# A third wide product in seven products of quarters, a weight loaded in halves, and a new instruction order

## The chip, the cores and the metric

The kernel runs on one core of a Trainium2 chip. The metric is the device time of one execution in microseconds. The core's engines are PE (matmul), DVE (vector), ACT (scalar), POOL (GpSimd, which here issues most loads) and SP (which issues stores and turning transfers).

## The reference

A recurrent retention layer is followed by a mixer over tokens and channels. B = 4 batches, H = 8 heads, S = 768 tokens, D = 64; the model width is 512, and the token and channel layers are 256 and 1536 wide. All inputs and the output are float32.

```python
gamma = 1.0 - 2.0 ** (-5.0 - np.arange(H))
for t in range(S):
    state = gamma * state + np.einsum('bhd,bhe->bhde', k[:, :, t], v[:, :, t])
    y[:, :, t] = (1 / np.sqrt(D)) * np.einsum('bhd,bhde->bhe', q[:, :, t], state)
x = y.transpose(0, 2, 1, 3).reshape(B, S, H * D)
h = np.maximum(x.transpose(0, 2, 1) @ w_tok1, 0.0) @ w_tok2
u = x + h.transpose(0, 2, 1)
out = u + np.maximum(u @ w_ch1, 0.0) @ w_ch2
```

## The kernel before, in words

Everything is held on the chip in 16-bit floats where matmuls read it. The work has two parts.

The **front** goes over 16 units, a batch b and a pair of heads p. The recurrence is cut into six chunks of 128 tokens. k and q are scaled by powers of the decay (L528 on ACT, L530 on DVE), turned by PE (L552, L554; the turned q of batch 0 and a few others is scaled at L562 with a table made at L433) or by a transfer on SP (L542). PE multiplies k and v into chunk states (L584), DVE runs the recurrence over the chunks (L594, L596), and the states go to the `cross` tiles (L614 on ACT, L616 on DVE). Scores (L635) are masked by DVE (L646, 128 x 384 at a time), and y is the masked scores times v (L666) plus the cross part (L692). Banks are evicted to 16 bits at L708 on ACT or DVE. The two token products are L723 and L743, with a rectification between them on ACT (L732) or DVE (L734). The result u is turned (L788 or a transfer at L778) into `uT`.

The **back** goes over batches. The wide product, u times w_ch1 with rectification, has two forms. `widen` makes 12 x 2 blocks of four matmuls over 384 tokens (L822), each rectified by ACT (L838). `widen7` splits both operands into quarters and makes seven products in place of eight: four differences of uT on DVE (L861), four sums of the weights made once, and then for each of six blocks seven products of two matmuls (L891), three copies of partial banks (L902, ACT or DVE), three additions on DVE (L911) that are rectified in place (L915, DVE), and one last rectification straight from the bank (L942 on ACT or L944 on DVE). The set `WIDE7` says which batches take this form; before, they are 2 and 3. The narrow product, with w_ch2, takes seven products for all batches (L1005 sums on DVE, L1041 and L1051 products, L1031 copies, L1058 additions), except the last half of batch 3, which is plain (L967, L976). Stores are issued at L982 and L1084.

The order is not found at run time. A planner (`arrange`) reads two strings: `ORDERED` names every operation once, in the sequence in which it is put on its engine, and `WAYS` says for operations that two engines can do which of them takes it (0 the first named, mostly ACT, 1 DVE). The class `Rings` models transfers with a time per descriptor, a first delay and a delay until landing; its numbers settle the order in which the emitted instructions of different engines and the banks are arranged. Each engine then runs its own instructions strictly in that order. Loads are all on POOL's queue except the first k, in the sequence that the string gives; from the seventh load on, a load waits for the one six places ahead of it. While the plan shows PE waiting in the first 21 us, filler matmuls on zeros are emitted (L1164).

The second token weight (256 x 768) is one load of two row tiles and is waited for by both halves j of the product at L743:

```python
t2 = op(one("PE", (335, 500), emit), [hr, wops["t2"], x_ops[j]], [], [H1, Y[j]])
```

Of the kernel before, what the change touches and what calls it, by code (L numbers as in the profile page):

```python
# [38 lines left out]
class Rings:  # L39
# [28 lines left out]
    def step(self, landed):  # L68
        dt, t = self.DT, self.t
        on = [(q, l[0]) for q, l in self.line.items() if l and l[0][2] <= t]  # L70
        if on:
            round_ = sum(x[0].dma[1] for _, x in on)
            for q, x in on:
                n = dt / round_
                if x[3] > t:
                    n = min(n, dt / self.GEN[q])
                x[1] -= n
                if x[1] <= 0:
                    self.line[q].pop(0)
                    landed.append((x[0], t + dt + self.land(q, x[0], t)))  # L80
        self.t = t + dt
# [9 lines left out]
def arrange(ops, BUFS, BANKS, seq, ways):  # L91
# [162 lines left out]

ORDERED = (
    "0b0d000a08050e0107020c2423040j060f292a030i2b250927260h282h2i2k0g332c2m342j0l352l37362d0k2e47382f2o2g0m43482q"
    "2n443h3i3k0n493l454a4b463m0q392p4c3a4h0o3j534d2r3b4k544e2s4i3c4f3d0p2t4j4g3e4l3f0s572u4m553g4n583n564o4p3p3o"
    "3q3r5i3s0u5l2v2y5m2w3t4r2x0v2z593u4q5a305h5b3v0t4s5c3y5d3w4t5e5j5f0w6763644u315k5g5o4v0r3z3x5n5p325q4w855r40"  # L260
    "0x4y4x86415s654z5t420z6650515u6894520y5v955y5w69115z6h5x76606j61hm1362hj6lij6ahn6k12hkim7372hp6b6ihlik106chq"
    "hsil6d77hrht74hois6e75786fithu79in7a147g7bioi4iu7jj16g7c6n7ihvhw7h6mj27ki5177d6oi77ei6iy6q1zhyhx6pi86rja21j3"
    "jgjh7f18206si9jijb6ti11c8182iv6ujciz6v6xig226yidi26w15hzi3iwi0jdihix83ia84ibj41aj01viej5iiip6z1w70j616j7icje"
    "if1yjn711987jj7m7o88iqjljo7lj81gjkir7nkb89j91xjfjp9z1b8ajukc7pjqaxjs8b1e7q8cjv8fk5jt8djy8i908gjw91k77r8hjxa0"
    "kgjm7s8ja18ek1khb0b18k7tjz8mk28l7u8njr7w1fb2k0a57x96kr8okk1d7v97ksk98pkl7y1h9892a6kaa28q93k61ukv99a78ra87z9a"
    "kwa9kea3809ba4aa8sk89cl0ay8tkt9eazkf9d8v9gkil19f8wkx9i8x9h8u9jl4kjctku9l9kky9m9n1ib3kdkn9ob4abb58ycu1sb69p8z"
    "b7kol21jb89qbvl5byadackz1ml39rag9u9sl9ae1t9vafl69wah9t9xl7bb9yaiajbfakal1nldbcamlelaanmdbdljbzmempc0mfaolfb9"
    "maapcvlkban4mqbeaqmrn5arcwbhm1bwbjasatbxllbgbiaumy1kmbn6kqavczc1mc1om2bkc2m7c3mzd0bldrmjepn0m8c4d1m3mkl8bmm9"
    "mlcxd2lyeq1lcybnmvkmlzlg1rd3bolbc5d4mwawbpbrmxlhbqm4k4dsm5k3bsc6mglibtlvm0lsd5m6c9eslmcdlwfnmhcblxlnlpcalolq"
    "ccltlrc7d7lummc8d8msd6mtcfdbmnn1etmod9njeumuminankn7ndcedtn2da1pn8nbnen9cgo5duncnfn3ddcidfcholevcjdxo6ordydv"  # L270
    "dzckdwe0glosnhewfoexe1noerclningdcnmey1qnpe2decmomnncpdgnlopcnezdhf0nqgmcqoonscrcsconrondie3ntoqfpnvf1djf2e5"
    "nwbuoufqe4e6dke8ovdnlce9dloynye7dmkpf3donzozowotdqdpf7eaebo1edeco3oxeef6p0eff4frf5ftegnuf9fup3o0nxeho4fso2f8"
    "faeip4o8p7ejp6p1fcfbgro7ekoafvo9fwfdgsocp9gtelfxodobfegup2ohffp8gooegvemoifgfyeneoofpbfhgwfjogpcpsfzfig1ptpg"
    "g4fkpdg5pxphpipepypjg2pzpkq0papufmplq1pqg0qqq2pngxpvgnq7q4flpoq9q8q5qgqrqxg3qaqvgyprqsqwqeqbqtqfqygpr7qcqzqh"
    "gqg6r0g8qir5gag7r2qjokr6g9ror3gbqlr9r8qmrercr1rppfqorardrqqdojrtpmr4rfqururrgcrgq3rwrhrvrxrmripwgdrjryqps3rn"
    "rbgerss4rzghqks0rkgfthtdgitjgjtfgktis1gggztesvh1tmh2srtoh0sws9tntph3h4tqqnssh6h5rlh7h8stt0q6h9tkt2t1tltrtss2"
    "tghattpptvtuhbt4s5hcs6t5hfhdt3sxs7hgt6s8sahihhsehet7sysbp5susgsfszsiscsht9t8sjsksdtbtzsnslsmu3uku0u4u5ulsoum"
    "u1u8upunu9uau6uqurubu2ustaucviutv8uduiuoufuuuzuguwv1vjuxvktwvnv2uvv3tyuevovlv6spvpv4v7vqtxv0vzvrv9wnvsvavxuj"
    "v5w1vbvuvywgvvvdvgvmw0vew6vhytw4w2whylwiu7w5w3wlvcuhymwjw7wmy5uyw8vwwowky6w9wpwevtwbwqwfwvvfsqwswrwcxnwwwtx1"
    "wdwuwaynxpxjxkyoxox3wxypxsxlx2wyyqxuxtxqxmxwx4x6wzxxxvx8x7xyx9yrydx0xaxzxcy0xby7x5y3y8xdysxfxetcy1xgxhy9xiy2"  # L280
    "yaxryey4yfybygyhyiycyuyvywyjyxyyykyzz0"
)
WAYS = (
    "000000000000000000000000000000000000000000000000000000000000000000000000000100000000000010000000000000100001"
    "001000000000000000000000000000000001101000000000000000000000000100100000100000000000000000000000000000000100"
    "001100000000000100000000000000011000001000000000001000000000000000000000010000000000000000000000000000000000"
    "000000000000000000000000000000000010001100000000000000000000010100000010010000000010000000000001001001011011"
    "000000010000000000100100100001100100000001100000000000000000000110110000000000000000000000000000010011000000"
    "010000000000000000100001001000000000000000000000000000000010010000000010000000000000000000000000000000000000"
    "000000000000000000000000000000000000000000000000000000000000000000000000000100000000000000000000011000000000"  # L290
    "000000000001100000000000000000000000000000000000000000000000000000000000000000000000000000000000000000000110"
    "000000000000000000001000000000000000000001100000000000000000000000000000000000000000000000000000000000001000"
    "000000000000000000000000000000000000000000000000000100000000010000000000000000000000100000000000000000000110"
    "000000000000000000000000000000000000000000000000000000000000000100000000000000000000000000000000000000000000"
    "0000000100000000011000000000000000000001000000001000000010000000100000001"
)


# [1 line left out]
def kernel(  # L300
# [74 lines left out]
    def one(eng, cost, emit):  # L375
        return [(eng, cost[0], cost[1], emit)]
# [122 lines left out]
    def front(b, p):  # L499
# [238 lines left out]
        for j in range(2):  # L738
            def emit(j=j):
# [62 lines left out]
    def back(b):  # L802
# [150 lines left out]
        def narrow(sh, blocks=range(HC)):  # L953
            H2, rel = H2s[sh], rels[sh]
            for i in blocks:
# [3 lines left out]
                for cols in cuts:  # L959
# [20 lines left out]
                    def emit(e, sh=sh, i=i, cols=cols):  # L980
                        t0 = (sh * HC + i) * P
                        (nc.sync if e == "SP" else nc.scalar).dma_start(out=out[b, t0:t0 + P, cols], in_=X.tile[:, sh * HC + i, cols])  # L982
                    op(either(emit, ACT=(380, 101), SP=(450, 100)), [ad], [], [X], dma=(8, 90 * w_ // C))


        def narrow7(i0, i1):
# [95 lines left out]
            for i, d in ((i1, [o21, o22]), (i0, [o11, o12])):  # L1082
                def emit(e, i=i):
                    (nc.sync if e == "SP" else nc.scalar).dma_start(out=out[b, i * P:(i + 1) * P, :], in_=X.tile[:, i])  # L1084
                op(either(emit, ACT=(380, 101), SP=(450, 100)), d, [], [X], dma=(8, 90))
# [8 lines left out]
        for f in steps:  # L1094
# [1 line left out]
            part[0] += 2  # L1096


    ORDER = ("q00 k00 q01 v00 k01 k02 k03 v01 v02 q02 q03 t1 t2 v03 k10 q12 q10 k11 q13 q11 a0 v10 a1 v11 "
             "a3 a2 b1 b2 b0 k12 v12 k13 v20 v13 k20 q20 q21 v21 k21 k22 k23 v22 q22 q23 v23 k30 v30 q30 "  # L1100
             "k31 v31 q31 v33 v32 k33 q32 k32 q33").split()
    for what in ORDER:
        n = int(what[1])
        if what[0] in "kqv":
            load(n, int(what[2]), what[0])
        elif what == "t1":
            weight("t1", 48, 40, wt1, moe_w_tok1)
# [36 lines left out]
    for b in range(B):  # L1144
        back(b)

    seq = [int(ORDERED[2 * i:2 * i + 2], 36) for i in range(len(ORDERED) // 2)]
# [49 lines left out]
```

## Time and profile before

| | |
|---|---|
| median of 3 runs | 189.81 us (189.17 to 190.44) |
| profiled execution | 190.01 us |
| its span, first to last instruction | 188.2 us |
| busy PE / DVE / ACT / POOL | 181.2 / 166.5 / 124.2 / 52.8 us |
| mean granted clock of PE | 0.999 |

Busy time counts an instruction from start to end, and the next one on the engine can start before that end; so the sum of single durations is larger than the busy time, and a matmul row that is busy all the time does not say that the matmuls run at their peak. The rows are read by line number of the kernel, as in the description above; `L822 PE MATMUL ... x192 | 36.0, 326` means 192 matmuls of line 822, 36.0 us busy together, 326 ns from start to end of one.

### The profile page before, as it was taken

The numbers are of one execution on the slowest core, as the hardware profiler recorded it, in microseconds if no ns is written. First come the engines' busy times: TensorE is split into PE (matmuls) and PEld (weight loads), VectorE is DVE, ScalarE is ACT, GpSimd is POOL, SyncE is SP. The second block draws the span as 40 slices with busy tenths as digits, with TensorE's granted clock in tenths as the row PEclk, the third lists the DMA queues.
The fourth block names the chain that finished last, engine by engine and source line by source line (L and its number), as shares of the span: only waits on it lengthen the run. The fifth ranks groups of instructions, "written<-read, shape, count | busy, mean of one in ns | idle before, by whom it ended". The sixth has DMA issues, their size and how long they took to land.

```text
span 188.2 us, 5284 instructions
## 1 busy us (share of the span) xinstructions
PE 181.2 (96%) x2109; PEld 136.7 (73%) x2109; DVE 166.5 (88%) x448; ACT 124.2 (66%) x282; POOL 52.8 (28%) x62
## 2 busy tenths in 40 slices
PE   7989999999999999999999899999999999999993
PEld 3455888667688988776668788965678986567872
DVE  3789999997889999958799989999999999999982
ACT  3965989569889898478663686598883444575100
POOL 7995686536440708405202200000000000000000
PEclk9999999999999999999999999999999999999999
DMA  9999999999999999999999979724312031121045
GB/s 122 155 157 196 179 188 177 208 191 201 159 155 144 125 155 122 147 136 163 195 163 127 115 99 251 158 43 86 98 56 45 0 101 56 72 98 59 0 177 215
DMA packets 91977, 24.92 MB, mean 132 GB/s; under 512 B 81968, under 2 KB 89008, under 8 KB 91952
## 3 DMA queue, kind: packets, MB, share of 16 engines
q0 software_dynamic: 67456, 13.18, 85.3%
q1 hardware_dynamic: 23776, 10.10, 24.5%
q10 hardware_dynamic: 720, 1.31, 1.9%
q8 instruction: 16, 0.26, 0.6%
q14 instruction: 9, 0.07, 0.1%
HBM read 26.74 MB, written 6.29 MB: 175 GB/s over the span
## 4 chain that ended last, share of the span: by engine, by line
PE 78%; DVE 12%; DMA 3%; ACT 2%; issue 2%; POOL 1%; SPq 0%; POOLq 0%; ACTq 0%; DVEq 0%
PE bank L822 16%; PE bank L891 15%; PE bank L1041 14%; PE bank L1051 10%; PE bank L743 5%; DVE am L646 4%; PE bank L723 4%; PE bank L635 3%; PE bank L967 3%; DMA kT<-k 3%; DVE U L596 2%; PE bank L666 2%; PE bank L692 2%; DVE qT L562 2%; PE bank L584 1%
## 5 line engine op out<-in xcount | busy, mean ns | idle before, releaser
L822 PE MATMUL bank<-uT,wc 128*128 128x384 f16 x192 | 36.0, 326 | 0.0
L646 DVE TENSOR_TENSOR am<-bank,mask 128x384 f16<-128x384 f32 x64 | 33.2, 549 | 1.7 <-PE bank L635 1.5
L838 ACT ACTIVATE h<-bank 128x384 f16<-128x384 f32 x48 | 21.5, 500 | 10.3 <-PE bank L822 10.3
L490 POOL DMA_DIRECT2D v<-in_v_dram x16 | 16.4, 1031 | 40.0 <-PE bank L692 17.9
L822 PEld LDWEIGHTS <-wc 128*128 128x128 f16 x192 | 17.2, 98 | 9.1 <-DVE X L708 0.2
L902 ACT COPY us<-bank 128x384 f32<-128x384 f32 x34 | 15.5, 481 | 8.9 <-PE bank L891 6.4
L1041 PEld LDWEIGHTS <-hs 128*128 128x128 f16 x198 | 18.5, 98 | 3.0 <-issue 0.7
L1031 ACT COPY us<-bank 128x256 f32<-128x256 f32 x31 | 11.8, 384 | 13.3 <-PE bank L1041 13.0
L911 DVE TENSOR_TENSOR h<-bank,us 128x384 f16<-128x384 f32 x36 | 19.3, 553 | 1.1 <-PE bank L891 0.4
L1058 DVE TENSOR_TENSOR X<-X,bank 128x256 f32<-128x256 f32 x44 | 17.9, 414 | 2.2 <-PE bank L1051 1.4
L1041 PE MATMUL bank<-wsum,hs 128*128 128x256 f16 x132 | 17.9, 273 | 0.6 <-ACT us L1031 0.6
L596 DVE SCALAR_TENSOR_TENSOR U<-U,gp,bank 128x64 f32<-128x64 f32 x64 | 17.1, 281 | 0.7
L708 ACT CAST x<-bank 128x384 f16<-128x384 f32 x30 | 14.1, 492 | 5.0 <-PE bank L692 5.0
L490 POOL DMA_DIRECT2D k<-in_k_dram x15 | 15.4, 1035 | 5.3 <-DVE U L596 1.7
L708 ACT CAST u<-bank 128x384 f16<-128x384 f32 x28 | 13.2, 489 | 3.4 <-PE bank L743 3.2
L891 PE MATMUL bank<-hs,late 128*128 128x384 f16 x72 | 14.9, 326 | 0.0
L743 PE MATMUL bank<-h,wt 128*128 128x128 f16 x192 | 14.7, 219 | 0.0
L891 PEld LDWEIGHTS <-late 128*128 128x128 f16 x96 | 9.0, 98 | 6.4 <-issue 0.4
L1051 PEld LDWEIGHTS <-h 128*128 128x128 f16 x132 | 12.5, 98 | 1.6
L614 ACT ACTIVATE cross<-U,gp 64x320 f16<-64x320 f32 x23 | 12.8, 560 | 1.2 <-DVE U L596 0.7
L723 PE MATMUL bank<-x,wt 128*128 128x128 f16 x192 | 13.3, 219 | 0.0
L743 PEld LDWEIGHTS <-wt 128*128 128x128 f16 x192 | 11.9, 98 | 1.6
(89 smaller groups left out, 374.2 us busy)
## 6 DMA issues: line engine op xcount, KB each, us to landing
out_dram<-X SPq DMA_DIRECT2D x18, 256.0 KB, 2.4
v<-in_v_dram POOLq DMA_DIRECT2D x16, 192.0 KB, 6.7
q<-in_q_dram POOLq DMA_DIRECT2D x16, 192.0 KB, 7.3
k<-in_k_dram POOLq DMA_DIRECT2D x15, 192.0 KB, 7.2
wc<-in_moe_w_ch_dram POOLq DMA_DIRECT2D x5, 512.0 KB, 13.4
out_dram<-X ACTq DMA_DIRECT2D x5, 256.0 KB, 2.1
wt<-in_moe_w_tok_dram POOLq DMA_DIRECT2D x2, 384.0 KB, 9.1
wc<-in_moe_w_ch_dram POOLq DMA_DIRECT2D x2, 256.0 KB, 9.0
```

Of the source, the lines that this page charges most:

```text
L490: (nc.sync if hard else nc.gpsimd).dma_start(out=tile_of(s, [P, 2, NC, D], FP if hard else F16), in_=src.rearrange("h (c p) d -> p (h c) d ...
L596: nc.vector.scalar_tensor_tensor(out=u[:, c], in0=u[:, c - 1], scalar=gp[:, p:p + 1], in1=st, op0=ALU.mult, op1=ALU.add)
L646: nc.vector.tensor_tensor(am, SC[g].tile[:, :m * P].rearrange("p (i t) -> p i t", t=P), mask.to_broadcast([P, m, P]), ALU.mult)
L708: (nc.scalar.copy if e == "ACT" else nc.vector.tensor_copy)(tile(), t)
L723: nc.tensor.matmul(acc[:, jt * P:(jt + 1) * P], wt1[:, i, jt * P:(jt + 1) * P], X16.tile[:, i].rearrange("p h d -> p (h d)"), start=(i == ...
L743: nc.tensor.matmul(Y[j].tile[:, 2 * i * D:2 * (i + 1) * D], wt2[:, jt, t], H1.tile[:, jt], start=False, stop=(jt == NJ - 1), skip_group_ch ...
L822: nc.tensor.matmul(acc[:, :SH], wc1[:, ct, ft * P:(ft + 1) * P], UT.tile[:, ct, sh * SH:(sh + 1) * SH], start=(ct == 0), stop=(ct == NP - 1))
L838: nc.scalar.activation(H2.tile[:, ft], A.tile[:, :SH], AF.Relu)
L891: nc.tensor.matmul(acc[:, :SH], left(ct), r[:, ct], start=first and ct == 0, stop=ct == C2 - 1, skip_group_check=True)
L911: nc.vector.tensor_tensor(h(m, sh), R.tile[:, :SH], KS.tile[:, j], ALU.add)
L1041: nc.tensor.matmul(acc_[:, lo], l[:, j], r[:, j], start=first and j == 0, stop=j == K2 - 1, skip_group_check=True)
L1051: nc.tensor.matmul(acc_[:, lo], l[:, j], r[:, j], start=first and j == 0, stop=j == K2 - 1, skip_group_check=True)
```

## The change

`WIDE7` becomes (1, 2, 3), so batch 1's wide product is made by `widen7`. The second token weight is loaded by two transfers of 384 columns each (`t2a`, `t2b`), and half j of the product waits for its own. The transfer model gets other numbers: a landing delay for ACT's queue, 700 instead of 1000 ns more for turning transfers, other landing delays for POOL's loads, POOL's share of the transfer engines fixed at 0.6 while a hardware queue is active, and 130 instead of 90 ns per descriptor of a store. `ORDERED` and `WAYS` are replaced as a whole (1296 operations in place of 1261; the two characters of an operation now count to base 62).

```diff
-    LAND = dict(SP=900, ACT=2000)
+    LAND = dict(SP=900, ACT=900)
-    LATER = 1000
+    SOFT = 0.6
+    LATER = 700
...
-            return 1470 if t < 6000 else 2900 if t < 13500 else 2300
+            return 1470 if t < 4500 else 2100 if t < 17000 else 1700 if t < 30000 else 2000
...
-            round_ = sum(x[0].dma[1] for _, x in on)
+            hard = len(on) - ("POOL" in dict(on))
             for q, x in on:
-                n = dt / round_
+                share = (self.SOFT if hard else 1.0) if q == "POOL" else (1.0 - self.SOFT if hard < len(on) else 1.0) / hard
+                n = share * dt / x[0].dma[1]
...
-    WIDE7 = (2, 3,)
+    WIDE7 = (1, 2, 3,)
...
-            t2 = op(one("PE", (335, 500), emit), [hr, wops["t2"], x_ops[j]], [], [H1, Y[j]])
+            t2 = op(one("PE", (335, 500), emit), [hr, wops["t2" + "ab"[j]], x_ops[j]], [], [H1, Y[j]])
...
-                    op(either(emit, ACT=(380, 101), SP=(450, 100)), [ad], [], [X], dma=(8, 90 * w_ // C))
+                    op(either(emit, ACT=(380, 101), SP=(450, 100)), [ad], [], [X], dma=(8, 130 * w_ // C))
...
-        elif what == "t2":
-            weight("t2", 16, 150, wt2, moe_w_tok2)
+        elif what[:2] == "t2":
+            half = slice(0, SH) if what == "t2a" else slice(SH, S)
+            weight(what, 16, 64, wt2[:, :, half], moe_w_tok2[:, half])
```

Read by number, the two orders differ in these places that the prediction speaks of. POOL's queue begins with v, q of the first unit, then k, q of the second, the iota of the decay table, q of the third; afterwards it begins with q, v of the first unit, that iota, then q, k, v of the second. DVE makes all constants before the first scaling of k. The first weights of the wide product stand behind two more loads of batch 1 (its first v and second k). Choices between engines: of 48 scalings of k and q, 26 were on DVE and 13 are; of 96 evictions at L708, 14 and 8; of 16 rectifications between the token products, 5 and 1; the last rectifications of `widen7`, 0 of 12 and 4 of 18; two copies of partial banks leave DVE. The last operations of the old order are plain narrow products in slices, the last of 128 columns, each with its store; in the new order these slices come earlier, and the last are a chain of seven-product matmuls, its addition and the store of a whole block of 128 x 512.

More of the change, by code (lines that the diff above doesn't have):

```diff
@@ L262 @@
[L262 to L266, printed above, removed]
@@ new lines @@
+    "1Y1z1q250n2o1r2s2p261B0k242q2t1A2u1C2r2v1D0p1Z2C2w201E2E2F0q2Y2x2D271F210r2y292G282Z2b2z2a2H0w2c342A1G2d3035"
+    "2B360t2I1H1J2e311I0s371K32382f392J1L332K2g2M0v2L1M3a2h2j2N1N3c0u2k2O3e2i3y2l3d3f0A4K2P3b3h3C3g3i3z3k2m3D0x3m"
+    "3j3l2Q3n2T4L0y2R3E3o2U3F3G2n5j0z3p47483q2V3t3H3r2W2S0D493u3I3A2X3v3w3J3saf0B3x3Bac5kadaMaeaN4aagaO3M4b3K3Q0C"
+    "ax3Naoap3Oay3Paq0EarazaV4caWahasaX0F3S4l3Lal4nat4d4o3R3T4eb74m3Vai4f0G3U4gaj4pamb84haG4ib9aD1aakauaE3WaA1c0L"
+    "avaHaw1b3XaFaJ3Y1daKaBaL3Z4j0JaIba4042bj4143bgaCaY4kanbk44bhbmb4bl0K1645bd46aZ18bb0Ibibeb54G4H4qbnaPbc174s0O"
@@ new lines @@
+    "bfb1b0aQaS19aR4M0Hb6b24I4Nb34OaTbo4ubO0Nbp4J4r4Pbq5f4QbPbsaU0M4Rbr4SbI4U5O4t4Wbv0R4v4Ybxbw4V5g4w0S4X4T6pbzbJ"
+    "5Pby500P4x5h6UbAbBbL5ibt4ZbK4y6q0Q5152bu4zbE534A5lc45U54bMbC6m5m5n4B6V5VbFbT5R5W5o555XbN5p4C5YbUbR5q6n5rbXbD"
+    "4Dc85Z56bYbS5S5tc5c95T5s575ucd585w4E5Qc7cebV595v4F5abQ6rchc6bW5x5y5Aci60c06o5C615b5z5BbZ0T6s5Dcm7sc16t5E0W5c"
+    "6u7tc36vcf7ucn5F0U6w626xcg6y5G636W155J5H645dcj655Kc25I66675L5Mck695e6A5N686bcl6aca6c6B6Xcqcu7v6dcb6EcvcLcc6e"
+    "cw6zcrcNcs6fcMcz6C6gcQ7wcA6i6DcBcRcOcC6Y70cxcDcT0Z6Zct6jcScU6GcEcJ6h0X6IcVcGcKcPd26k71cHcX0V80dR72cYd4d3dT73"
@@ new lines @@
+    "12dScyd7d57yd8dUdWd97zdVdXda7AcF6F746HdbdZ7B11756Jd07CdcdYe0dh6K7D13cIde76e1e6df6L14e7did1dj6Me3dkcW78e48y6Q"
+    "7983dA7adodBdl8zdpdC7b8AdF77dmdrdG7cdHdsdqbGdD7d7EdI7xdtdydJdE7edn7ge5dz6N0YdubHdK81dPdvdd6Oe2dM82dLdQd67fdw"
+    "867Feyeu6RdNeU6Pew7heWev7i6SeF87cZez88eQ847jeG85eDdxdg7kdO96eSeJ99896leReAeEeX9a7leK7oeB9b7meH8a8b7nex7G8ceT"
+    "f1eI8d7KeM7J7pf2eVee7r7qeN97e8eZef8B7Mco7If58C98eCf07H8e7O8gf3cp8i8D7L7NeLf4ec107Pf6f87Q6Te9ed8f8E7R8hf98j8l"
+    "7Seaeh9E8Feg8k8n8mf77Tei7WeY7Uej8G8oeb7X9cekel7V7Z9d7Y8H9een9fem8I9F9g8peo9G8Jeq9h8qep8K8Meres8L8r8Q8u8s8P8N"
@@ new lines @@
+    "8t9k8vfcfg8wfx8O8xfhfdfzfy8R9o8T9Hfl9mfC8V8SfAfm8UfifefD9K8W9lfofF9nfp8Xfj9ifn9Lff8YfEfGfqfv9Ig5fHfsfw9JfMft"
+    "fJfNfQ9MfKg6fOg79NfPfBga9O9pfRfTgb8Z9PfU9jgdeOgcg89Q9qfWfu90ge9r92fXfVgf9t9sgkfY93gh9uglg39591g0gi949vg1g4gm"
+    "9R9wgDfkgnfI9SgEgr9TgIgs9U9xgKfZ9y9WgugJgFfSg9gtgv9VgL9zgwgBgM9XfrgogggCgN9ZgSa1gpgygT9YgOa0gx9Agza2gPhChGhE"
+    "a3hHhDhNgQa49BhLgRgGhIhOhMgqgHa5fLhghPhFhkhihQa6a8g2hJhrgAa9hhhlhUabhKgjhRhsaahp9DhVhSgYgUhqhmhTgVh0gZa7gWh3"
+    "9Ch1hjhvh4hnh5hwhohth2h6h7gXh9huh8hxhyhahchAhYhbi2ijhZi3i4hdikj8i0i7iohzi8ili5hBipiqimiahfi9i1etibirePiAicis"
@@ L1084, in emit @@
                     (nc.sync if e == "SP" else nc.scalar).dma_start(out=out[b, i * P:(i + 1) * P, :], in_=X.tile[:, i])
-                op(either(emit, ACT=(380, 101), SP=(450, 100)), d, [], [X], dma=(8, 90))
+                op(either(emit, ACT=(380, 101), SP=(450, 100)), d, [], [X], dma=(8, 130))
         if b in SEVEN:
@@ L1102 @@
     for what in ORDER:
-        n = int(what[1])
+        n = int(what[1:2])
         if what[0] in "kqv":
@@ L1145 @@
         back(b)
-    seq = [int(ORDERED[2 * i:2 * i + 2], 36) for i in range(len(ORDERED) // 2)]
+    digit = {c: i for i, c in enumerate(DIGITS)}
+    seq = [digit[a] * 62 + digit[c] for a, c in zip(ORDERED[::2], ORDERED[1::2])]
     asked = set(o.n for o in queue)
```

50 lines of the change are left out of this document (18 added, 32 removed).

## The prediction

> **What bounds the kernel now.** I read the page's span and chain, then the busy time in five stretches that I cut at the first useful matmuls of a stage, then groups and timelines for the price of one instruction.
>
> ```profile
> span 188.2 us, 5284 instructions
> PE 78%; DVE 12%; DMA 3%; ACT 2%; issue 2%; POOL 1%; SPq 0%; POOLq 0%; ACTq 0%; DVEq 0%
> ...
> 0.00:10.00 10.00, 8.54 (x63) 4.35 (x64) 5.30 (x37) 6.50 (x11) 8.86 (x15) 1.00 1.27 140
> 10.00:33.40 23.40, 21.87 (x402) 17.48 (x401) 22.36 (x53) 18.68 (x38) 16.72 (x21) 1.00 1.86 180
> 33.40:78.40 45.00, 44.88 (x557) 34.94 (x555) 41.03 (x102) 35.84 (x82) 20.19 (x20) 1.00 1.92 161
> 78.40:156.50 78.10, 77.42 (x877) 60.01 (x875) 71.07 (x189) 51.32 (x125) 7.06 (x7) 1.00 0.78 115
> 156.50:188.20 31.70, 28.44 (x218) 19.94 (x215) 26.70 (x69) 11.92 (x28) 0.00 (x0) 1.00 0.26 96
> ```
>
> The columns are the stretch and its length, then PE, weight loads, DVE, ACT, POOL, clock, DMA share and GB/s. The profiled execution took 190.01 us, 1.8 above its span, and lies 0.2 above the median 189.81. Three regimes are to be seen. Until 33.4 us DVE is the full engine (22.36 of 23.40) and PE is kept busy by filler (39 matmuls, 10.1 us, row below). From 33.4 to the end PE is full (44.88 of 45.00, then 77.42 of 78.10). The granted clock is 1.00 throughout. So matmul time removed after 33.4 us counts in full as long as DVE and ACT keep up. DVE is close behind: from 78.4 to 156.5 us it is idle for 7.0 us only, ACT for 26.8.
>
> ```profile
> L822 PE MATMUL bank<-uT,wc 128*128 128x384 f16 x192 | 36.0, 326 | 0.0
> L1164 PE MATMUL bank<-zero 128*128 128x384 f16 x39 | 10.1, 411 | 1.1 <-DVE zero L1155 1.1
> L911 DVE TENSOR_TENSOR h<-bank,us 128x384 f16<-128x384 f32 x36 | 19.3, 553 | 1.1 <-PE bank L891 0.4 <-ACT us L902 0.2
> L915 DVE TENSOR_SCALAR h<-h 128x384 f16<-128x384 f16 x36 | 7.6, 251 | 0.0
> L838 ACT ACTIVATE h<-bank 128x384 f16<-128x384 f32 x48 | 21.5, 500 | 10.3 <-PE bank L822 10.3
> L646 DVE TENSOR_TENSOR am<-bank,mask 128x384 f16<-128x384 f32 x64 | 33.2, 549 | 1.7 <-PE bank L635 1.5
> L528 ACT ACTIVATE k<-k,gk 128x384 f16<-128x384 f16 x17 | 10.0, 613 | 2.5 <-DMA kT<-k 2.2
> L902 ACT COPY us<-bank 128x384 f32<-128x384 f32 x34 | 15.5, 481 | 8.9 <-PE bank L891 6.4 <-DVE h L911 2.5
> ...
> 33.41 3.58 PE bank L822 x22
> 94.92 0.87 ACT L838 ACTIVATE h<-bank 128x384 f16<-128x384 f32 x2 [0.16 <-PE bank L822]
> 8.85 1.12 ACT L528 ACTIVATE k<-k,gk 128x384 f16<-128x384 f16 x2
> 142.10 1.01 DVE L646 TENSOR_TENSOR am<-bank,mask 128x384 f16<-128x384 f32 x2
> 139.09 0.76 DVE L915 TENSOR_SCALAR h<-h 128x384 f16<-128x384 f16 x4
> 67.80 0.32 DVE L530 TENSOR_SCALAR k<-k,gk 128x384 f16<-128x384 f16 x1
> 68.03 0.55 DVE L1005 TENSOR_TENSOR hs<-h 128x768 f16<-128x768 f16 x1
> ```
>
> **Steps, not durations.** An engine starts its next instruction before the last has drained, so I price by the step from start to start. A 384-column matmul: 3.58 us for 22 in the chain, 0.163. A DVE instruction over 128x384 from a bank: two take 1.01 and one 0.55, 0.46 to 0.47; the in-place rectification L915: (0.76 - 0.25) / 3 = 0.17; a decay L530: 68.03 - 67.80 = 0.23. On ACT an eviction: 0.87 - 0.50 = 0.37; a decay: 1.12 - 0.61 = 0.51.
>
> **The change, part by part.**
>
> *The wide product of batch 1.* It goes from 12 x 2 blocks of 4 matmuls (96) to 6 blocks of 7 products of 2 (84). All have 384 columns, so PE loses 12 x 0.163 = 1.96 us. DVE gains 4 sums and 18 additions at 0.47 and 18 rectifications at 0.17: 10.3 + 3.1 = 13.4 us. ACT loses 24 evictions (8.9) and gains 18 copies (6.7).
>
> *The engine choices.* Read number by number, the second string takes 13 decays, 6 evictions, 4 small rectifications and 2 copies from DVE to ACT, and puts 4 rectifications and a few turned tiles on DVE. Over the kernel DVE gains about 8.4 us of steps and ACT about 7.5.
>
> *The stretch in which it falls.* From the first wide product of batch 1 to that of batch 3 both orders hold the same work but for the exchange, so they can be set side by side. PE: 77.6 us of steps before and 75.7 after (the trace's stretch is 78.1). DVE: 67.1 before; +8.4 additions, +3.0 rectifications, +1.4 sums, +0.9 last rectifications, -2.7 for 12 decays, -1.9 for 4 evictions, -1.9 for 4 of the cross tiles and -1.1 for small ones give 73.3. ACT: 45.8 to 53.8. With PE's saving the stretch would be 76.1 us, of which DVE must step 96.3%. Has it done that? In the two rows below DVE was busy for 9.53 and 9.94 of 10 us while PE was full, 97.4%.
>
> ```profile
> 110.00:120.00 10.00, 10.00 (x158) 8.51 (x156) 9.53 (x24) 6.96 (x19) 0.00 (x0) 1.00 0.86 188
> 120.00:130.00 10.00, 10.00 (x99) 7.26 (x98) 9.94 (x27) 8.28 (x21) 0.00 (x0) 1.00 0.42 94
> ```
>
> The loss to a late DVE is therefore 0 at best. By busy time, where drains count, it is 7.0 idle - 6.2 added - 1.96 shorter = 1.2 us too little. I take +0.5, with 0 and +1.2 as its ordinary ends; beyond them lies the first rival. What waits on a late DVE: in a block the fourth product waits for an addition to free its bank, and later blocks take banks that the additions and ACT's copies release, so PE stops with a few blocks' lag.
>
> *The front.* Here DVE decides. The new order loads q of the first head pair first on POOL's queue, moves the second iota ahead of the next loads, makes the constants first and turns k and q before the first state product.
>
> ```profile
> 5.28 0.53 DVE L530 TENSOR_SCALAR k<-us,gk 128x384 f16<-128x384 f32 x1
> 5.62 2.50 ACT L433 ACTIVATE late<-us,lnsc,lnh 128x384 f32<-128x384 f32 x4
> 6.51 0.80 DVE L416 TENSOR_SCALAR ident<-away 128x128 f16<-128x128 f32 x1
> 8.43 0.96 DVE L562 TENSOR_TENSOR qT<-bank,late 128x768 f16<-128x768 f16 x1 [0.49 <-PE bank L552]
> 9.82 0.56 DVE L646 TENSOR_TENSOR am<-bank,mask 128x384 f16<-128x384 f32 x1 [0.43 <-PE bank L635]
> ```
>
> The decay table L433 starts at 5.62 because its iota stands behind four loads; in the new order it stands behind two, and the scaling L562 at 8.43 could start about 0.9 earlier. Against that the second pair's k is issued one load later (three take POOL 3.05 us in a row shown with the last rival, so about 1 us each), and a decay of it waiting on ACT holds the next copies: up to 1.5 us the other way. DVE's steps before the first wide product are nearly equal (27.2 and 27.5). I take -0.7, ends -0.9 and +1.5.
>
> *The second token weight in halves.* One more issue on POOL (L470, some 0.8 us, its rows below) delays the loads behind it by that. Its cover is the lead of those loads: the first wide product starts at 33.41 and its first weights were issued at 18.71, with 9.0 us to landing. They land by 27.7, a lead of 5.7 us. In the new order they stand behind two further loads of 192 KB, at the stretch's 180 GB/s 2.2 us. That is inside the lead: cost 0, and if the cover goes +0.8.
>
> ```profile
> 18.71 0.77 POOL L470 DMA_DIRECT2D wc<-in_moe_w_ch_dram  x1 [1.35 <-DMA wt<-in_moe_w_tok_dram]
> wc<-in_moe_w_ch_dram POOLq DMA_DIRECT2D x2, 256.0 KB, 9.0
> ...
> 182.26 2.68 PE L967 MATMUL bank<-wc,h 128*128 128x512 f16 x24
> out_dram<-X SPq DMA_DIRECT2D x18, 256.0 KB, 2.4
> out_dram<-X SPq DMA_DIRECT2D x2, 64.0 KB, 1.8
> ```
>
> *The end.* Before, PE ends on narrow slices (L967) and the last store is one of 64 KB, 1.8 us to landing. The new order ends on a seven-product chain, a 256-column addition and a whole 256 KB block, 2.4 us. That is +0.6 for the store and +0.1 for the addition: +0.7, ends 0 and +1.0. The new costs in the transfer model (stores, landing) act only through the order.
>
> **Sum**, on the profiled span: 188.2 - 1.96 - 0.7 + 0.5 + 0.7 = 186.7; with 1.8 around it 188.5, and 0.2 less against the median: **188.3 us**, 0.8% below 189.81. About 1% is what a measurement of this kernel tells from no change, so that forecast lies just inside it.
>
> **Rivals.**
>
> *DVE becomes the bound (slower).* Place: 78 to 156 us. In the old stretch DVE was busy for 91% (71.07 of 78.10). If its chains (addition, rectification, the next sum) allow no more than that, 73.3 us of steps need 80.5, 4.4 more than PE's 76.1. It decides from a share below 96.3%. Sum: 188.2 - 1.96 - 0.7 + 0.7 + 4.4 + 1.6 = 192.2. For it: all spare DVE time of the stage is spent. Against: the two rows above.
>
> *Nothing comes of it.* DVE loses the 1.2 and the front gains nothing: 188.2 - 1.96 + 1.2 + 0.7 + 1.6 = 189.7. For it: in 10 to 33.4 us DVE had one idle microsecond, so an earlier start may only meet later loads.
>
> *Stalls go as well (faster).* The old trace has one costly order: ACT stands 2.25 us for a turned k, and a copy queued behind it holds PE.
>
> ```profile
> 98.80 5.15 DMA kT<-k
> 104.05 1.12 ACT L528 ACTIVATE k<-k,gk 128x384 f16<-128x384 f16 x2 [2.25 <-DMA kT<-k]
> 105.47 0.82 PE L1041 MATMUL bank<-wsum,hs 128*128 128x256 f16 x6 [0.60 <-ACT us L1031]
> ```
>
> If the new transfer costs place it better and DVE keeps up: 188.3 - 0.6 - 0.5 = 187.2, with the front at its end and a free tail 186.3. Against it: 13 more decays now stand on ACT, each such a place.
>
> *Decay and rectification against POOL.* A decay usually takes 0.31 us on DVE, but up to 0.81.
>
> ```profile
> 73.44 3.05 POOL L490 DMA_DIRECT2D k<-in_k_dram  x3
> 73.76 0.81 DVE L530 TENSOR_SCALAR k<-k,gk 128x384 f16<-128x384 f16 x1
> 78.40:100.00 21.60, 21.60 (x227) 14.55 (x225) 17.11 (x47) 14.82 (x35) 5.53 (x6) 1.00 1.42 164
> ```
>
> The slow one ran while POOL issued three loads. The 18 new rectifications are of the same form and now fall where POOL still issues, as none did before. At 0.5 us each and POOL busy for 5.53 of 21.60 us, about a quarter, that is 18 x 0.25 x 0.5 = 2.3 us on DVE, 190.6 in all; the 13 decays that leave DVE give part back. The Trainium skill (SBUF — State Buffer, Who interferes with whom) says that such one-input DVE instructions in a two-port mode and GpSimd's descriptor writing take a shared port from each other for a whole instruction; this row agrees, while other decays beside POOL's issues took 0.3.
>
> **Chances.** The forecast with its own range 187.4 to 189.2: 0.47, of which 0.15 is below the 1% mark. Stalls go as well: 0.22, all below it. Nothing: 0.12. The DVE bound: 0.14, of which 0.11 beyond 1%. POOL's port: 0.05, of which 0.01 beyond. Faster by over 1%: 0.37; within: 0.51; slower: 0.12. The range, 186.2 to 191.6, leaves out the worst of the DVE bound and the best of the stalls.
>
> **What would show it.** Right: 96 matmuls left of L822's form and 252 of L891's; the stretch from the first wide product of batch 1 to that of batch 3 near 76.5 us with DVE busy above 95% and PE waiting under 1.5 us for DVE; the first mask multiplication at or before 9.3 us, the first wide product by 33; a last store of 256 KB. Wrong: PE waiting for additions or copies by several us in that stretch (DVE bound), the first wide product after 34 us (late loads), L915 above 0.4 us in the mean (port), or ACT waits on turned tiles longer than 2 us.

## The result and the profile after

The changed kernel takes **190.74 us** (median of 20 runs, 188.91 to 194.09) and the kernel before 189.22 (20 runs, 188.84 to 190.44). The ratio is 1.0045 with a 95% interval of [1.0024, 1.0066]: 0.45% slower, within the 1% called no change, where the forecast 188.3 was a gain. Four executions of the changed kernel, each over 1.5% above its fastest, are left out of the ratio; without them its median is **190.07 us**, and later medians are set beside that. The profiled execution took 191.62 us, 1.55 above 190.07; its span is 189.8, its mean granted clock 0.994. So the profile is one of the longer executions. Seven of the twenty took 188.91 to 189.53, and no profile is of one of those. Every line number of the front and of `widen7` is now three higher (L822 is L825).

The page of the changed kernel, span and chain by engine; then its busy time in stretches cut as before (stretch, length, PE, weight loads, DVE, ACT, POOL, clock, DMA share, GB/s):

```profile
span 189.8 us, 5308 instructions
PE 75%; DMA 8%; ACT 5%; POOL 5%; DVE 3%; issue 1%; SPq 0%; POOLq 0%; ACTq 0%
```

```profile
0.00:32.95 32.95, 30.12 (x449) 21.26 (x450) 27.94 (x94) 23.23 (x48) 25.89 (x36) 1.00 1.64 169
32.95:80.50 47.55, 45.26 (x574) 35.18 (x573) 42.81 (x101) 37.00 (x85) 18.68 (x19) 1.00 1.92 151
80.50:156.60 76.10, 75.92 (x859) 58.18 (x857) 74.61 (x205) 60.30 (x144) 9.10 (x9) 1.00 0.95 104
156.60:189.80 33.20, 28.97 (x224) 20.60 (x222) 27.20 (x71) 11.81 (x27) 0.00 (x0) 0.97 0.34 128
```

The third row is the one that the forecast was about: 76.10 us long where the old was 78.10, DVE busy for 98% of it, PE full. The second is the surprise: it was 45.00 us long with PE busy for all but 0.12; now it is 47.55 with PE idle for 2.29. In the chain DMA has gone from 3% to 8%.

The costly groups of the changed kernel (busy us, mean ns of one, idle before):

```profile
L825 PE MATMUL bank<-uT,wc 128*128 128x384 f16 x96 | 17.7, 326 | 0.0
L894 PE MATMUL bank<-hs,late 128*128 128x384 f16 x108 | 22.5, 326 | 0.1
L894 PE MATMUL bank<-uT,wc 128*128 128x384 f16 x72 | 15.6, 326 | 0.0
L894 PE MATMUL bank<-uT,late 128*128 128x384 f16 x36 | 8.8, 326 | 0.0
L894 PE MATMUL bank<-hs,wc 128*128 128x384 f16 x36 | 8.6, 325 | 0.0
L914 DVE TENSOR_TENSOR h<-bank,us 128x384 f16<-128x384 f32 x54 | 28.9, 550 | 1.2 <-ACT us L905 0.4 <-PE bank L894 0.2
L918 DVE TENSOR_SCALAR h<-h 128x384 f16<-128x384 f16 x54 | 12.2, 264 | 0.0
```

The change does what it says: 96 wide matmuls are left and 252 (108 + 72 + 36 + 36) stand in seven-product chains, 12 fewer in all. The rectification takes 264 ns against 251.

**Where the 2.3 us of this execution went.** The timeline of the changed kernel around 72 us, SP's and POOL's queues and PE's row after the stop:

```profile
66.95 2.46 SPq L545 DMA_TRANSPOSE qT<-q  x1
69.46 1.27 SPq L545 DMA_TRANSPOSE kT<-k  x1
70.78 1.28 SPq L545 DMA_TRANSPOSE qT<-q  x1
72.11 5.97 SPq L545 DMA_TRANSPOSE kT<-k  x3
...
71.74 1.01 POOL L493 DMA_DIRECT2D v<-in_v_dram  x1 [9.80 <-PE bank L695]
72.74 1.08 POOL L493 DMA_DIRECT2D q<-in_q_dram  x1
73.81 1.01 POOL L493 DMA_DIRECT2D k<-in_k_dram  x1
74.81 1.03 POOL L493 DMA_DIRECT2D q<-in_q_dram  x1
...
79.04 0.51 PE L638 MATMUL bank<-qT,kT 64*128 64x128 f16 x12 [2.24 <-DMA kT<-k]
```

Its chain of waits and its list of waits at this place:

```profile
72.11 6.89 DMA kT<-k
```

```profile
PE bank L638 <- DMA kT<-k: 2.2, 1, 2.2
```

SP's own longest wait is the other half of it, with the DVE instruction that it waited for:

```profile
SPq L545 <- DVE q L533: 65.7, 1, 65.7
```

```profile
66.53 0.32 DVE L533 TENSOR_SCALAR q<-q,gy 128x384 f16<-128x384 f16 x1
```

SP's queue stands until 66.95 before a q whose scaling DVE makes at 66.53. The 65.7 us of the row run from SP's first load on, for that q is next on its queue. With that q six turning transfers of batch 2 go out one behind the other, 1.3 to 2.5 us apart. The k of the second head pair is the fourth, issued at 72.11; it takes 6.89 us to land, beside a store of ACT and four loads that POOL issues between 71.74 and 75.8 after its own queue has stood for 9.80 us. PE's scores of that pair wait 2.24 us for it, and everything behind them on PE with them. Before, the same stage turned fewer tiles at a time and from 60 us on (DVE scaled that q at 60.82); SP's queue there, and the time to landing of the four k turned from 55 to 84 us:

```profile
60.01 2.09 SPq L542 DMA_TRANSPOSE kT<-k  x1
62.21 6.10 SPq L542 DMA_TRANSPOSE qT<-q  x2
68.37 1.28 SPq L542 DMA_TRANSPOSE kT<-k  x1
```

```profile
kT<-k SPq DMA_TRANSPOSE x4, 3.1
```

The same row of the changed kernel:

```profile
kT<-k SPq DMA_TRANSPOSE x4, 8.3
```

The Trainium skill (DMA: Bandwidth & Descriptors, Queues, rings and completion order) says that each transfer engine takes turns between the queues it has work for. The rows fit this but do not show the turns themselves: the k issued at 69.46 landed after 2.84 us, the one issued at 72.11, beside the loads and the store, after 6.89.

### The profile page after: what moved, and what is told of

It is laid out like the page before. It is cut to its first block, busy times and chain, and to the rows that moved or that the text cites. A ratio compares the mean times of both kernels' runs of the same rounds, so it can differ in the third digit from the quotient of the medians.

```text
span 189.8 us, 5308 instructions
## 1 busy us (share of the span) xinstructions
PE 180.3 (95%) x2099; PEld 135.2 (71%) x2099; DVE 172.5 (91%) x470; ACT 132.3 (70%) x300; POOL 53.7 (28%) x63
## 3 DMA queue, kind: packets, MB, share of 16 engines
q10 hardware_dynamic: 1152, 1.77, 2.5%
## 4 chain that ended last, share of the span: by engine, by line
PE 75%; DMA 8%; ACT 5%; POOL 5%; DVE 3%; issue 1%; SPq 0%; POOLq 0%; ACTq 0%
PE bank L894 17%; PE bank L1044 14%; PE bank L1054 10%; PE bank L825 8%; PE bank L746 5%; PE bank L726 5%; DMA k<-in_k_dram 5%; DMA kT<-k 4%; PE bank L638 3%; PE bank L970 3%; ACT us L905 2%; PE bank L669 2%; PE bank L695 2%; DVE h L914 2%; POOL v L493 2%; PE bank L587 2%
## 5 line engine op out<-in xcount | busy, mean ns | idle before, releaser
L905 ACT COPY us<-bank 128x384 f32<-128x384 f32 x54 | 24.8, 482 | 8.0 <-PE bank L894 5.1
L914 DVE TENSOR_TENSOR h<-bank,us 128x384 f16<-128x384 f32 x54 | 28.9, 550 | 1.2 <-ACT us L905 0.4
L1034 ACT COPY us<-bank 128x256 f32<-128x256 f32 x30 | 11.2, 375 | 16.7 <-PE bank L1044 15.2
L894 PE MATMUL bank<-hs,late 128*128 128x384 f16 x108 | 22.5, 326 | 0.1
L894 PEld LDWEIGHTS <-late 128*128 128x128 f16 x144 | 12.7, 98 | 7.6 <-issue 0.5
L825 PE MATMUL bank<-uT,wc 128*128 128x384 f16 x96 | 17.7, 326 | 0.0
L599 DVE SCALAR_TENSOR_TENSOR U<-U,gp,bank 128x64 f32<-128x64 f32 x64 | 16.3, 273 | 0.6
L894 PE MATMUL bank<-uT,wc 128*128 128x384 f16 x72 | 15.6, 326 | 0.0
L531 ACT ACTIVATE k<-k,gk 128x384 f16<-128x384 f16 x22 | 13.3, 619 | 2.5 <-DMA k<-in_k_dram 2.2
L894 PEld LDWEIGHTS <-wc 128*128 128x128 f16 x108 | 10.1, 98 | 5.9 <-issue 0.3
L711 ACT COPY X<-bank 128x384 f32<-128x384 f32 x29 | 13.7, 500 | 0.2 <-DVE u L711 0.2
```

The lines of the kernel that those rows point to most:

```text
L599: nc.vector.scalar_tensor_tensor(out=u[:, c], in0=u[:, c - 1], scalar=gp[:, p:p + 1], in1=st, op0=ALU.mult, op1=ALU.add)
L711: (nc.scalar.copy if e == "ACT" else nc.vector.tensor_copy)(tile(), t)
L825: nc.tensor.matmul(acc[:, :SH], wc1[:, ct, ft * P:(ft + 1) * P], UT.tile[:, ct, sh * SH:(sh + 1) * SH], start=(ct == 0), stop=(ct == NP - 1))
L894: nc.tensor.matmul(acc[:, :SH], left(ct), r[:, ct], start=first and ct == 0, stop=ct == C2 - 1, skip_group_check=True)
L905: (nc.scalar.copy if e == "ACT" else nc.vector.tensor_copy)(ks[:, j], R1.tile[:, :SH])
L914: nc.vector.tensor_tensor(h(m, sh), R.tile[:, :SH], KS.tile[:, j], ALU.add)
```

## The experiments

Each edit is against the changed kernel if nothing else is said. The characters of the order string stand for operations, two for each.

**The two kernels again, unchanged.**

> The kernel before, unchanged, looked at once more. Its first profile took 190.01 us where the median of 20 executions is 189.22, and held a stop of 0.8 to 1.0 us on PE at 104.2 to 105.5 us behind a turning transfer of 5.15 us. Theory 'transfers decide the odd microsecond': an execution near 189.2 us has that transfer at about 3 us and PE stops under 0.3 us at that place. Rival 'the stop is part of the order': the stop is there again at 0.8 us or more in an execution of 189.2 us.

> The changed kernel, unchanged, looked at once more. The profiled execution (191.62 us) stopped PE for 2.4 us at 76.6 us, for a turned k that took 6.9 us. Theory 'collision': the time of an execution follows that stop, so one of 189.0 to 189.5 us has a stop of under 0.5 us there and one above 191 us of 2 us or more; the stretches after it are the same within 0.3 us. Rival 'DVE is the bound': the stop is the same size whatever the time, and the difference lies between 80 and 157 us, where DVE is full.

Measured: 190.54 us (span 188.8) and 191.82 us (span 190.0). The starts of the first matmuls of each stage cut the profiled executions into these parts (us; W is the first wide product of batch 0, at L822 or L825, w1 and w3 those of batches 1 and 3):

| kernel | start to W | W to w1 | w1 to w3 | w3 to last matmul | to the end |
|---|---|---|---|---|---|
| before, first profile | 33.25 | 45.01 | 78.21 | 28.25 | 3.49 |
| before, second | 34.58 | 45.01 | 77.45 | 28.25 | 3.49 |
| after, first | 32.78 | 47.71 | 76.81 | 27.99 | 4.55 |
| after, second | 33.51 | 47.11 | 76.82 | 28.00 | 4.58 |

PE's stop of about 2 us ahead of L638 is in both profiles of after (2.24 and 1.6 us in the waits) and in none of before. What the old trace had of its own, the stop of 0.6 us behind ACT's turned k at 104 us (0.76 by the stretch), is not in its second profile. Yet that second execution is the longer one: PE waits 1.2 us for the first token weight (L723), and the front takes 34.58 us. Neither of the two executions lies near its kernel's median, so what was expected of one that does is not decided by them. An old execution put together from the parts without these two stops is 33.25 + 45.01 + 77.45 + 28.25 + 3.49 = 187.45 us and 1.8 around it, 189.25: that is the median of 189.22. The forecast's base, 189.81 from three runs, was 0.6 too high, and its profile held a stop that the second profile lacks.

**loads_early**: three POOL loads ahead of the one that waits.

```diff
-    "...5BbZ0T6s5Dcm7sc16t5E0W5c"
-    "6u7tc36vcf7ucn5F0U6w626xcg6y5G636W155J...
+    "...5BbZ0U0W150T6s5Dcm7sc16t"
+    "5E5c6u7tc36vcf7ucn5F6w626xcg6y5G636W5J...
```

> Three loads of batch 3 (k and q of the first pair, q of the last) are taken ahead of the load of v that stood on POOL's queue for 9.8 us, so that they run while the transfer engines are nearly idle (66 to 71 us) and not in the burst from 71.7 us on beside the turned k. Theory 'collision with the loads': the turned k takes about 3 us, PE's stop at 76.6 us goes from 2.4 to under 0.5 us, and the median falls from about 190.5 to 188.7 to 189.2 with a spread of under 1 us. Rival 'the turns hold each other': the k still takes above 5 us and the median stays above 190. Rival 'DVE is the bound': the stop goes, and what it gave comes back as waits after 80 us, median above 190.

Measured: 190.37 us (189.54 to 191.77), ratio to before 1.0039 [1.001, 1.0067]. In its profile the k of the second pair takes 5.2 us instead of 6.9, and no PE wait on it is listed; but that execution took 189.72, and the median is no lower than 190.07. Taking the burst away shortens the transfer, it does not bring the time back.

**turns_late**: two of the six turns (k of the fourth and third pair, `7u`, `6W`) behind a store on SP.

```diff
-    "6u7tc36vcf7ucn5F0U6w626xcg6y5G636W155J5H645dcj655Kc25I6...
+    "6u7tc36vcfcn5F0U6w626xcg6y5G63155J5H645dcj655Kc27u6W5I6...
```

> On SP's queue the turned k of the fourth and third pair of batch 2 are put behind the store that followed them, so that the turned k that PE waits for is not followed at once by two more. Theory 'collision with the loads': little changes, the k still takes 5 us or more, median 190 to 191. Rival 'the turns hold each other': the k falls to about 3 us, the stop goes, and the median is 188.7 to 189.3.

Measured: **189.09 us** (188.85 to 191.27), ratio 0.9989 [0.9961, 1.0017]. k takes 5.1 us. One edit of SP's order takes 0.98 us off the median (190.07). Four of the twelve executions still take 189.96 to 191.27.

**turns_tail**: turns_late with the old ending (the whole last block ahead of the last slice).

```diff
-    "iCfbieit...j9j4kMj6...
+    "iCfbieit...j9j4kwj6...
...
-    "kektjHkJkOjR...kjjUkQkRkmjYjWkSjXk8kTjZkwk0kxk9k1kykzkakAkBkkkCkDklkn"
+    "kektjHkJkyjR...kjjUkAkBkmjYjWkCjXk8kDjZkkkMk0kNk9k1kOkPkaklknkQkRkSkT"
...
```

> On top of the order with the two turned k behind the store (189.09 us): the last seven-product chain of batch 3 is put ahead of the last six slice matmuls, with its addition and its store of 256 KB, and the 128-column slice comes last, as in the kernel before. In the changed kernel 4.5 us lie between the start of the last matmul and the end of the span, before 3.5. Theory 'the end costs 1 us': the distance falls to about 3.5 to 3.8 and the median to 188.1 to 188.4. Rival 'PE's end moves instead': the distance falls, but the last matmul starts later by as much, median 188.9 to 189.3.

Measured: 188.89 us, ratio 0.9991 [0.9961, 1.0022], but from two groups of executions: six at 188.45 to 188.89 and five at 189.93 to 191.52. The profile is one of the upper group: it shows the stop again, 1.7 us, with k landing in 6.5 us. The way from the last matmul's start to the end is 4.2 us in it, where 3.5 to 3.8 was expected. So an order that turns the k late by a hair seems to lose the race in part of its executions, and a median of a dozen runs can fall on either side; that the lower group has no stop is inferred from turns_late's profile (189.18 us, no wait).

**turns_loads**: both edits together.

> Both moves together: the two turned k behind the store, and three loads of batch 3 ahead of the waiting load of v. If the loads of the burst still slowed the turned k, it now lands in under 4 us (5.1 with the turns alone moved) and the times scatter less than 188.85 to 191.27, median 188.9. Rival, after the 190.37 us of the loads alone: loads run early cost by themselves, since the transfer engines are then busy when the turns of q and the loads of batch 2 run, and the median is 190 or more.

Measured: 189.69 us (189.05 to 190.92), ratio 1.0016 [0.9996, 1.0036]; k lands in 4.7 us, the shortest of these, and yet the median is 0.6 above that of turns_late. The two ratios' intervals overlap, so a cost of the loads moved forward is not shown; nor is there a sign that the two edits add.

**turns_t2_whole**: turns_late with the second token weight in one transfer again.

```diff
-            t2 = op(one("PE", (335, 500), emit), [hr, wops["t2" + "ab"[j]], x_ops[j]], [], [H1, Y[j]])
+            t2 = op(one("PE", (335, 500), emit), [hr, wops["t2"], x_ops[j]], [], [H1, Y[j]])
...
```

The order strings name the same sequence with one load less.

> On top of the order with the two turned k behind the store: the second token weight is one load again, at the place of the first half. Theory: the halves neither give nor cost, median within 0.3 us of 189.1. Rival 'the extra issue delays the loads behind it': 0.5 us faster. Rival 'the first half comes early enough to matter': 0.3 to 0.8 us slower, with the first wide product after 33.3 us (now 32.9).

Measured: 190.06 us (188.99 to 193.54), ratio 1.005 [1.002, 1.008], 0.97 above turns_late, whose interval lies lower throughout. The timelines, first of this kernel, then of turns_late:

```profile
22.20 0.51 PE L746 MATMUL bank<-h,wt 128*128 128x128 f16 x6 [0.90 <-DMA wt<-in_moe_w_tok_dram]
```

```profile
21.41 0.51 PE L746 MATMUL bank<-h,wt 128*128 128x128 f16 x6
```

In one piece the weight makes PE wait 0.90 us, and the first wide product starts at 33.71 instead of 32.93. Both kernels issue the load, or its first half, at 12.10 us; the whole lands at 22.15, the first half at 21.10. The Trainium skill (Perfetto Trace Analysis, DMA Optimizations) says that splitting transfers into smaller ones may let some of them start sooner. Here the half starts at the same time and lands 1.05 us sooner.

**turns_old_wide**: turns_late with batch 1's wide product in blocks of four matmuls again (`WIDE7 = (2, 3,)`; the operations from there on in an order made new for it, everything earlier unchanged).

> On top of the order with the two turned k behind the store: batch 1's wide product is made in four products again (48 half blocks put at the places of the 42 products, each rectified by ACT), the rest of the order and the choices between engines as in the changed kernel. It has 12 more matmuls of 384 columns, 1.96 us of PE, and 13.4 us less on DVE. Theory 'half of the saving is lost to a late DVE': from the first wide product of batch 1 to that of batch 3 it takes 76.5 + 0.6 to 1.2 us and the median is 189.6 to 190.3. Theory 'the saving counts in full': 76.5 + 2.0, median 191. Rival 'DVE is the bound': 76.5 or less, median 189 or less.

Measured: 191.71 us, ratio 1.0141 [1.0102, 1.018]. The stretch from w1 to w3, first of this kernel, then of turns_late:

```profile
78.32:157.36 79.04, 78.50 (x878) 60.09 (x876) 62.43 (x167) 61.23 (x145) 9.10 (x9) 1.00 1.10 100
```

```profile
78.39:154.89 76.50, 76.41 (x865) 58.73 (x863) 75.42 (x208) 60.27 (x144) 9.09 (x9) 1.00 1.06 104
```

2.54 us longer, with DVE busy for 62.4 instead of 75.4 us. The 12 matmuls are worth 1.96 of it; the other 0.58 comes beside three stops that turns_late does not have (at 80, 91 and 103 us, 0.30 to 0.37 each). So, with the rest of the order as it is, the seven-product form is worth at least its 12 matmuls although DVE is nearly always busy.

**k_first**: both k of batch 2's first two pairs (`5Q`, `6o`) ahead of the first q (`5T`) on SP.

```diff
-    "4Dc85Z56bYbS5S5tc5c95T5s575ucd585w4E5Qc7...0c06o5C6...
+    "4Dc85Z56bYbS5S5tc5c95Q6o5T5s575ucd585w4Ec7...0c05C6...
```

> After's kernel with the turning transfers of batch 2 put in another order at the head of SP's queue: both k of the first two pairs go ahead of the first q, so that SP does not stand before the q until 66.95 us while k is ready, and the k of the second pair is no longer the fourth of a chain. Theory (the chain of four to six turning transfers, with ACT's store and the POOL loads beside its end, makes that k late): it is issued some us before 72.11, lands before the scores ask for it at 76.6, PE's stop of 2 us there is gone in every execution, the last matmul starts near 183.0, and the median is 188.9 to 189.1 with the upper runs near it. Rival (the transfers of this stretch are slow wherever they stand, because the loads and stores beside them take their share): another of the turned tiles, the q now behind, is late by 1 us or more, and the median stays at 190 to 190.7.

Measured: **188.95 us** (188.87 to 189.93; eleven of twelve at most 189.07), ratio 0.9987 [0.9971, 1.0003]. SP's queue and its transfers' time to landing from 55 to 84 us:

```profile
59.39 7.26 SPq L545 DMA_TRANSPOSE kT<-k  x2
66.86 3.36 SPq L545 DMA_TRANSPOSE qT<-q  x2
73.19 3.34 SPq L545 DMA_TRANSPOSE kT<-k  x2
```

```profile
kT<-k SPq DMA_TRANSPOSE x4, 8.1
qT<-q SPq DMA_TRANSPOSE x3, 4.6
```

The transfers are no faster in the median than without the edit (8.1 and 8.3 us for k); the two k that were moved take 7.2 and 5.4 us, where they took 2.8 and 6.9. They start earlier: at 59.39 the first k goes out that had stood behind the q until 69.46, and the second at 65.44 instead of 72.11. It lands at 70.8 instead of 79.0. PE waits for none of them, and all but one of the upper runs are gone. The theory holds for the order and the rival is right about the speed of a turn.

**k_first_tail**: k_first with the old ending, as in turns_tail.

> The kernel k_first, with the old ending as well: the whole last block of 512 columns is added and stored ahead of the last slice, and the last store is the slice of 128 columns. If the 1.06 us by which after's way from the last matmul's start to the span's end is longer (4.55 against 3.49) come from the whole block and its larger store at the end, that way is about 3.6 here and the median some 0.4 to 0.9 below that of k_first: 188.2 to 188.6, and faster than both kernels. Rival (PE only ends later by what the end saves, since the order of the last matmuls changes with it, or the store's time does not depend on its size): within 0.3 of k_first.

Measured: **188.70 us** (188.38 to 189.24), ratio to before 0.9965 [0.9948, 0.9982]; it is faster than both kernels, 0.3% under the one before. The way from the last matmul's start to the end is 4.18 us where k_first has 4.52, and 3.6 was expected; so the median falls by 0.25 only.

**rect_short**: k_first with the rectification of 64 of 384 columns only; the other 320 are left unrectified.

```diff
-                        nc.vector.tensor_scalar(h(m, sh), h(m, sh), 0.0, None, ALU.max)
+                        nc.vector.tensor_scalar(h(m, sh)[:, :64], h(m, sh)[:, :64], 0.0, None, ALU.max)
```

> The kernel k_first, with the separate rectification after each seven-product addition done on 64 of its 384 columns only (the other 320 are left as they are). 36 of these stand between the first wide product of batch 1 and that of batch 3; at about 0.27 us each they take 8.4 us of VectorE there, and should take about 0.1 each now, some 6 us less. In k_first this stretch is 76.55 us, 0.90 under the 77.45 of the kernel before in its second profile, though 12 matmuls of 0.163 us (1.96) are gone. Theory (the 1.06 that is lost again is TensorE kept back by VectorE, which is 98% busy there): the stretch falls to about 75.5 and the median to about 187.9. Rival (it is lost in the order of the matmuls, more changes from one kind to another, which VectorE does not set): the stretch stays within 0.3 of 76.55 and the median within 0.3 of 188.95.

Measured: 188.72 us (188.59 to 189.1), ratio to before 0.9968 [0.9957, 0.9978], 0.23 under k_first. The line L918 (min/median/max ns) of k_first and of this kernel, and the stretch from w1 to w3 of each:

```profile
L918 DVE TENSOR_SCALAR h<-h x54: 240/253/611, 84.3 to 172.1; 128x384 f16<-128x384 f16 x54
```

```profile
L918 DVE TENSOR_SCALAR h<-h x54: 170/174/718, 84.7 to 172.1; 128x64 f16<-128x64 f16 x54
```

```profile
78.11:154.66 76.55, 76.46 (x865) 58.72 (x863) 75.54 (x208) 60.31 (x144) 9.10 (x9) 1.00 1.00 105
```

```profile
78.54:154.82 76.28, 76.25 (x865) 58.82 (x863) 73.67 (x208) 60.20 (x144) 9.10 (x9) 1.00 1.01 104
```

A sixth of the columns still takes two thirds of the time (medians), so DVE was relieved by 1.9 us only, not by the 6 that the expectation counted on. The stretch gives back 0.27 of the 1.06 us. That is the rival's case by its own numbers, but the test was weaker than meant: it shows that 1.9 us less on DVE brings 0.27, not what 6 us would.

## Why the prediction was wrong

All its signs came true in the first profile, and the time went the other way. The first mask multiplication is at 8.92 us, in the rows of DVE's timeline:

```profile
8.92 1.02 DVE L649 TENSOR_TENSOR am<-bank,mask 128x384 f16<-128x384 f32 x2 [0.96 <-PE bank L638]
```

The first wide product is at 32.78 (in the second profile at 33.51, past the mark of 33), the stretch w1 to w3 at 76.81 with DVE at 98%, PE's waits there name no addition, L918 takes 264 ns, ACT waits for turned tiles 0.3 us in all. None of these signs looked at the stretch from 33 to 78 us.

**The step that failed** is the one that was not taken: the turns that the new order moves past each other on SP's queue had no price. The prediction read the choices of engines and POOL's loads number by number, but not SP's sequence, and put the stretch W to w1 at no change. Here are its rows, of before, after and k_first:

```profile
33.25:78.26 45.01, 44.89 (x558) 34.94 (x556) 40.89 (x102) 35.88 (x81) 20.19 (x20) 1.00 1.91 161
```

```profile
32.78:80.49 47.71, 45.42 (x576) 35.28 (x574) 42.87 (x102) 37.16 (x85) 18.84 (x19) 1.00 1.92 152
```

```profile
32.70:78.11 45.41, 45.36 (x576) 35.29 (x574) 42.17 (x101) 37.21 (x85) 18.48 (x19) 1.00 1.99 158
```

It grew by 2.70 us in the profiled execution; 2.30 of it is the stop that k_first takes away, and that alone is 190.07 - 188.95 = 1.12 in the medians, since not every execution has it. Forecast (-1.46) and measurement (190.07 - 189.22 = +0.85) are 2.3 apart: about half is this step, the other half the terms below. The rival "Stalls go as well" had the mechanism, a turned k that comes late, and the sign wrong: it quoted the old place at 104 us as something to win and named 13 decays on ACT as the counter-risk. The place where it struck was a decay of q on DVE that holds SP's queue, and PE's scores behind it.

**Term by term**, k_first against the execution before that was put together above (187.45 us of span), since k_first is the change without that stop:

| term | forecast | measured |
|---|---|---|
| front, to W | -0.7 | -0.55 |
| W to w1 | 0 | +0.40 |
| w1 to w3 | -1.96 + 0.5 = -1.46 | -0.90 |
| w3 to last matmul | 0 | -0.26 |
| end | +0.7 | +1.03 |
| sum | -1.46 | -0.28 |

-0.28 from 189.22 gives 188.94, and k_first has 188.95, so the parts add up. The first row is the least certain: between two profiles of one kernel W moves by 1.3 us (before) and 0.7 (after).

- *The matmuls.* Right: -1.96 is there (875 matmul starts in the stretch before, 863 after, by count of starts in the trace), and turns_old_wide shows it by itself.
- *Late DVE.* In size it was off: 1.06 where 0.5 was taken, inside the ends 0 and 1.2. The profile before, with its own stop of 0.76 in this stretch, made the forecast -1.46 look met (-1.40). The prediction's check that DVE can step 96.3% of the time took two rows where it was busy for 97.4%; but busy time has drains in it (in the old stretch its own 67.1 us of steps were 71.1 busy), so those rows did not show it. From the step of each matmul's start to the next, above the lower quartile of its own form, PE loses 5.28 us in the second profile before and 6.32 in k_first, with 112 and 122 changes from one line to another. Most of the difference stands at one place, where 12 scores take 0.73 us instead of 0.51:

```profile
118.18 0.51 PE L638 MATMUL bank<-qT,kT 64*128 64x128 f16 x12
119.39 0.73 PE L638 MATMUL bank<-qT,kT 64*128 64x128 f16 x12
120.12 1.25 PE L894 MATMUL bank<-uT,wc 128*128 128x384 f16 x6
```

From there to 121.7 us four steps are longer by 0.23, 0.20, 0.12 and 0.18, 0.73 together. PE goes on at 119.81 when a DVE mask is done, at 120.12 and 120.89 after ACT's evictions, at 121.67 after a DVE sum. The same four steps, to 0.01 us, are in rect_short and in turns_old_wide, with DVE relieved, and neither profile before has them. So the larger part is a place of the new order where PE meets masks, sums and evictions. It is not the rectifications, and it does not follow DVE's share of the stretch. No run moves that place alone.
- *The front.* The gain in the mark is there in these profiles, its worth is not. PE has 18 matmul rows more behind the mark W than before (576 against 558): work that stood ahead of it now follows, in a stretch 0.40 longer. The net is -0.15.
- *The halves* were set at 0, and are worth 0.8 us: without them the front would have been late. The term was sought in the wide weights' lead and not in the product that waits for the halves.
- *The end.* The sign is right, and +1.03 (+1.06 in the changed kernel) lies just past the upper end of 1.0. The last stores and their time to landing, before and after:

```profile
out_dram<-X SPq DMA_DIRECT2D x1, 64.0 KB, 1.7
```

```profile
out_dram<-X SPq DMA_DIRECT2D x1, 256.0 KB, 2.0
```

The store itself is 0.3 of it, not 0.6. Its issue comes 0.17 later behind the last matmul (184.72 to 185.31 before, 185.29 to 186.05 after), and by these times the span ends 1.23 us after the landing before and 1.77 after. Those 0.54 us are the largest part, and not the block's: in k_first_tail, which ends on 64 KB again, the span ends 1.72 us after the last landing. Why they differ is not shown.
- *The other rivals.* The DVE bound (192.2) did not come: the stretch ran at 98% DVE. "Nothing comes of it" (189.7, or 189.1 from a base of 189.22) is, without the stop, close in time but by other terms. POOL's port was feared at 2.3 us. It is there in small: in the first profile six of the 54 rectifications run beside POOL's loads, two of these take 674 and 604 ns and the other four 240 to 251. That is 0.8 us on DVE, and the mean of all is 264 ns.

## What to carry to other kernels

When an instruction order is replaced as a whole, compare every queue's sequence, the transfer queue of the idle-looking engine too. SP issued its transfers in their order here: a k that could go out at 59.39 us went out at 69.46, behind a q that waited for DVE. Set a first-come mark (such as "first wide product") beside the count of instructions on each side of it, or work that was only moved past the mark is booked as a gain. Take the base from many executions, and ask of each stop in the profile whether a second profile has it.

## What was not expected of the hardware

A turned k took 2.8 us to land with little beside it and 5 to 11 us as one of a chain beside POOL's loads. The changed kernel's executions spread from 188.91 to 194.09 us, and each of its profiled ones had such a k land after PE's need. A DVE instruction on 64 columns took 174 ns where 384 columns took 253 (medians). Of 54 rectifications of one form, two took over 600 ns, both while POOL issued a load. The first of two loads of 192 KB landed 1.05 us before one of 384 KB did, and the product that waits for it came forward by 0.8 us.
